# Part of VectorE's exponential on GpSimd, as int32 adds on pairs of int16 values, in a two-branch attention kernel

## The chip, the cores and the metric

The kernel runs on one core of one Trainium2 chip. The metric is device time in microseconds (us) of one execution; the median of several runs is quoted. The profile's own span, from the first to the last instruction, is about 1.8 us shorter than the measured time of the same run.

## The reference

Two attention branches over one sequence (S = 2048, D = 512, 32 heads of 16 columns) are mixed by a gate. All inputs are bf16.

```python
def reference(A_x, A_wqkv, A_wo, B_x, B_wqkv, B_wo, gate_w):
    def _A_ref(x, wqkv, wo):                     # full attention
        ...
        scores = jnp.einsum("bhqd,bhkd->bhqk", q, k) * scale
        p = _softmax(scores, axis=-1)
        o = jnp.einsum("bhqk,bhkd->bhqd", p, v)
        ...
    def _B_ref(x, wqkv, wo):                     # window of 8 keys, dilation 2
        ...
    x = A_x
    g = _sigmoid((x * gate_w).sum(-1, keepdims=True))
    a = _A_ref(x, A_wqkv, A_wo)
    b = _B_ref(x, B_wqkv, B_wo)
    return g * a + (1 - g) * b
```

The cost is in branch A: 32 heads x 2048 x 2048 scores must be exponentiated. The kernel cuts them into 2048 tiles of 128 x 512.

## The kernel before

The kernel holds a scheduler written in Python. While the program is built, it keeps a clock for each engine, picks what each engine does next from a list of steps with estimated durations, and emits that instruction. What runs on the chip is therefore one fixed order for each engine. Each score tile is given to one of two engines. ScalarE takes the true exponential of two or three tiles in one instruction. VectorE makes an approximation: it writes the score, scaled and shifted, as int16, whose bits read as fp16 are an exponential with a sawtooth error, and then two copies with another shift. The products with three differently weighted values average the error out.

```python
        def exp_dve(slot_item):                  # first step: one tile, from PSUM
            ...
            return nc.vector.tensor_scalar(out=self.yb[bt["buf"]][:, 0, i * 512:(i + 1) * 512], in0=bank[:],
                                           scalar1=A, scalar2=1024.0 * (15.0 + PW_S[0]), op0=ALU.mult, op1=ALU.add)

        def piece(bt, k):                        # second and third step: shifted copies of up to four tiles
            n = len(bt["items"]) * 512
            y = self.yb[bt["buf"]]
            return nc.vector.tensor_scalar(out=y[:, k, 0:n], in0=y[:, 0, 0:n],
                                    scalar1=float(round(1024.0 * (PW_S[k] - PW_S[0]))), scalar2=None, op0=ALU.add)
        ...
            for k in range(1, NP_):              # in close_batch: NP_ is 3
                s = Step("DVE", T_D4(n), lambda k=k: piece(bt, k), deps=list(bt["p1"]), due=bt["due"], cls=2)
                s.on_done = lambda end, k=k: done(k, end)
                s.port = True
                self.steps.append(s)
```

A step marked `port` is one that must not run beside GpSimd. The scheduler keeps such a step back while its clock for GpSimd is ahead, and makes each GpSimd instruction wait for the last of them:

```python
            if eng == "POOL" and port_last is not None:
                tc.add_manual_dep(inst.ins, port_last.ins.name, SYNC)
            if s.port:
                port_last = inst
```

```python
    def heads(self):
        pidx, pf, ei, ef = self.idx
        nc.vector.tensor_scalar(out=pidx[:], in0=pidx[:], scalar1=4, scalar2=None, op0=ALU.arith_shift_right)
        nc.vector.tensor_copy(out=pf[:], in_=pidx[:])
        nc.vector.tensor_copy(out=ef, in_=ei)    # 128x128, float32 from int32
        ...

    # elsewhere, where the steps are listed:
        self.steps.append(Step("DVE", 0.9, self.heads, rel=24, due=30, cls=2))
```

At the end each output tile of 128 rows is projected, cast into a staging tile of a rotating pool, and stored:

```python
        def ev():
            ob = self.wk.tile([P, D], BF16, name="ob", tag="ob")
            nc.vector.tensor_copy(out=ob[:], in_=self.misc[:])
            nc.sync.dma_start(out=self.o_dst[:, st, :], in_=ob[:])
```

Of the kernel before, what the change touches and what calls it, by code (L numbers as in the profile page):

```python
# [9 lines left out]
ALU = mybir.AluOpType  # L10
AX = mybir.AxisListType
ENG = mybir.EngineType
F32 = mybir.dt.float32
F16 = mybir.dt.float16
BF16 = mybir.dt.bfloat16
I16 = mybir.dt.int16
I32 = mybir.dt.int32
PSUM = bass.MemoryType.PSUM

P = 128  # L20
S = 2048
D = 512
# [19 lines left out]
NP_ = len(PW_S)  # L42
# [13 lines left out]
TUNE = dict(relL=64, dueL2=2040, R0=74, R1w=42, R1g=20, R2g=31, R3g=46, R3w=50, dueB=61, dueL=84, v2rel=79, v2step=21, v2due=91, krel=230, krel2=192, ahead=0.142, dueV=30, dueS=115, dueO=678, dlast=62, qrel=28, prelB=59, prodrel=-12)  # L56

LEVELS = dict(
    backlog=(0.758, 1.231, 1.61, 1.894, 2.273, 2.841, 3.788),
    backlog_s=(0.888, 1.442, 1.886, 2.219, 2.663, 3.329, 4.438),  # L60
    part_us=(0.6, 0.975, 1.275, 1.5, 1.8, 2.25, 3.0),
# [7 lines left out]
    order=((-1, 0, 1, 2, 1), (-1, 1, 0, 2, 3), (-1, 0, 2, 1, 3), (-1, 0, 1, 2, 3), (1, 0, 1, 2, 3), (0, 0, 1, 2, 3), (1, 0, 2, 1, 3), (2, 0, 1, 2, 3)),  # L69
)  # L70
STRETCH = dict(
    backlog="0333323133333333033333345336335333336333333333343333344333334633",
    backlog_s="0333333333333303331332333333333331333313430313333033333333333233",
    part_us="6333533463316323333303333303033333333333633463636333230333333333",
    misc_slack="3333333333333324333333433333333533332331033333333333333333333333",
    urgent="3333333333333333333333333333333333333333333353333363333333333333",
    fit="3533233333333333333133303333333333333333333330333333331333333363",
    port="1363353033333033333333333333333333335434353333333333333323533433",
    alone="3333333331363343333333333333333333133333333343333333631333333033",
    grab="0000000040000040000000004000000000004002000000000000000003000200",  # L80
    lend="0000000000060060000000000500020000000000000000000000200600060000",
    order="7001000330720000000000205000000000003000500010000000002000000002",
)
SLOT_D = 3
X_LAND = (0, 1.7, 3.7, 5.2)
# [631 lines left out]
T_D1 = lambda n: n / 960.0 + 0.075  # L717
T_D2 = lambda n: n / 1920.0 + 0.075
T_D4 = lambda n: n / 3840.0 + 0.075
T_P1 = lambda n: n / 750.0 + 0.1  # L720
T_P2 = lambda n: n / 480.0 + 0.06
MM = 0.216
SWITCH = 0.11
T_SP = 0.55
# [2 lines left out]
@with_exitstack  # L727
def kernel(
    ctx: ExitStack,
    tc: tile.TileContext,  # L730
    A_x: bass.AP,
    A_wqkv: bass.AP,
    A_wo: bass.AP,
    B_x: bass.AP,
    B_wqkv: bass.AP,
    B_wo: bass.AP,
    gate_w: bass.AP,
    out: bass.AP,
):
    nc = tc.nc  # L740
    aps = (A_x, A_wqkv, A_wo, B_x, B_wqkv, B_wo, gate_w, out)
    fpool = ctx.enter_context(tc.tile_pool(name="flag", bufs=1))
    flag = fpool.tile([P, 1], I32, name="flag")
    tc.mark_branch_hint_location("exact", hint="LikelyTaken", engines=[ENG.SP, ENG.Activation, ENG.DVE, ENG.PE, ENG.Pool])
    with ExitStack() as c1:
        _Fast(c1, tc, aps, flag).build()
    cond = nc.values_load(flag[0:1, 0:1], min_val=0, max_val=1)
    with tc.If(cond > 0, label="exact"):
        tc.strict_bb_all_engine_barrier()
        with ExitStack() as c2:  # L750
            _build_exact(c2, tc, aps)

class _Fast:
# [15 lines left out]
    def setup(self):  # L769
# [20 lines left out]
        self.t1 = c([P, 2, 16, 32], F32, name="t1")  # L790
        self.t2 = [c([P, 16, 32], BF16, name=f"t2_{i}") for i in range(2)]
        self.ident = c([P, P], BF16, name="ident")
        self.pmask = c([P, 2], F32, name="pmask")
        self.gw = c([P, 4], BF16, name="gw")
        self.gwr = c([P, 4, 32], BF16, name="gwr")
# [62 lines left out]
        for w, v, v4 in zip(PW_W[1:], self.vw[1:], self.vw4[1:]):  # L858
            nc.gpsimd.memset(v4[:, :, :, DH:VS], w)
            nc.gpsimd.memset(v4[:, :, 8, 0:DH], 0.0)  # L860
            nc.gpsimd.memset(v[:, len(KD) * H * VS:], 0.0)
        nc.gpsimd.memset(self.halo[:], 0.0)
        self.idx = pidx, pf, ei, ef
        nc.gpsimd.memset(self.ones[:], 1.0)
        for i in range(1, NQM):
# [571 lines left out]
    def outproj_specs(self, st):  # L1437
        nc = self.nc

        def mmh(srcs):  # L1440
            for br, ct in srcs:
                o = self.oT[ct] if br == "A" else self.oB(ct)
                w = self.woA if br == "A" else self.woB
                self.mm4(self.misc, lambda c: o[:, st * 128 + 32 * c:st * 128 + 32 * c + 32], w[:, ct, :],
                         start=(br == "B" and ct == 0), stop=(br == "A" and ct == 3))

        def ev():
            ob = self.wk.tile([P, D], BF16, name="ob", tag="ob")
            nc.vector.tensor_copy(out=ob[:], in_=self.misc[:])
            nc.sync.dma_start(out=self.o_dst[:, st, :], in_=ob[:])  # L1450
        order = [("B", c) for c in range(4)] + [("A", c) for c in range(4)]
        return [("PE", 2 * MM, lambda k=k: mmh(order[k:k + 2])) for k in (0, 2, 4, 6)] + [("DVE", T_D1(512), ev)]
# [30 lines left out]
    def run(self):  # L1483
# [39 lines left out]
        def tune(k):  # L1523
            return table[k][min(p, N - 1) * len(table[k]) // N]
# [23 lines left out]
        def ready_time(s):  # L1548
            r = 0.0
            for d in s.deps:  # L1550
                if d.end is None:
                    return INF
                r = max(r, d.end)
            return r
# [4 lines left out]
            return nc.vector.tensor_scalar(out=self.yb[bt["buf"]][:, 0, i * 512:(i + 1) * 512], in0=bank[:],  # L1559
                                           scalar1=A, scalar2=1024.0 * (15.0 + PW_S[0]), op0=ALU.mult, op1=ALU.add)  # L1560

        def piece(bt, k):
            n = len(bt["items"]) * 512
            y = self.yb[bt["buf"]]
            return nc.vector.tensor_scalar(out=y[:, k, 0:n], in0=y[:, 0, 0:n],  # L1565
                                    scalar1=float(round(1024.0 * (PW_S[k] - PW_S[0]))), scalar2=None, op0=ALU.add)

        def close_batch():
            nonlocal batch
            bt = batch  # L1570
            batch = None
            n = len(bt["items"]) * 512
            bt["refs"] = NP_ * len(bt["items"])
            parts = [dict(n=NP_) for _ in bt["items"]]

            def done(k, end):
                for i, it in enumerate(bt["items"]):
                    add_pv(it, self.yb[bt["buf"]][:, k, i * 512:(i + 1) * 512].bitcast(F16), end, ("y", bt, k), parts[i])
            for k in range(1, NP_):
                s = Step("DVE", T_D4(n), lambda k=k: piece(bt, k), deps=list(bt["p1"]), due=bt["due"], cls=2)  # L1580
                s.on_done = lambda end, k=k: done(k, end)
                s.port = True
                self.steps.append(s)
            last = bt["p1"][-1]

            def after(end, prev=last.on_done):
                prev(end)
                done(0, end)
            if last.end is None:
                last.on_done = after  # L1590
            else:
                done(0, last.end)

        def add_pv(it, rhs, ready, src, part=None):
            b, kt, j = it
            q = pvq[j]
            i = len(q)
            while i > 0 and q[i - 1][0] > b:
                i -= 1
            q.insert(i, [b, kt, rhs, ready, src, part or dict(n=1)])  # L1600
# [269 lines left out]
            return t["PE"] + 0.25  # L1870

        guard = 0
        while True:
            guard += 1
            assert guard < 2000000
# [13 lines left out]
                    moved = True  # L1889
            if p >= N and not self.steps and not aq and not any(pvq) and cur == NB:  # L1890
                break
            eng = min(t, key=lambda e: t[e])
            now = t[eng]
            others = min(v for e, v in t.items() if e != eng)
# [205 lines left out]
```

## Time and profile before

| | before |
|---|---|
| measured time, median of 3 | 714.39 us (714.26 to 714.79) |
| span of the profiled run | 712.4 us |
| busy: TensorE, VectorE, ScalarE, GpSimd | 689.5, 678.4, 691.3, 243.3 us |
| tiles: ScalarE, VectorE | 1492, 556 |
| last score round to the end of the span | 13.2 us |

In the profile PE is TensorE, DVE VectorE, ACT ScalarE and POOL GpSimd. A group's line has the source line, engine, operation, output and input names with shapes and the count, then after the bar the busy time in us and the mean duration of one in ns, then the idle time just before these instructions with what ended most of it.

### The profile page before, as it was taken

To read this page: it belongs to the slowest core of one execution; us is meant where nothing else is said; L and a number is where in the kernel's file an instruction comes from. 1 tells how busy PE (TensorE), PEld (TensorE's weight loads), DVE (VectorE), ACT (ScalarE), POOL (GpSimd) and SP (SyncE) were. 2 spreads that over 40 slices of the span, in tenths; PEclk is the share of its full clock that TensorE was granted. 3 is DMA by queue.
4 is the path that set the end of the run, shared out by engine and by line. 5 is a ranking of instruction groups with operands and counts; after the bars stand their busy time and mean duration, and the time that the engine had idled before them with its cause. 6 is when DMAs were issued, how large, how long until landed. Compare 5 with 4: busy or idle time off the path is not lost.

```text
span 712.4 us, 21197 instructions
## 1 busy us (share of the span) xinstructions
PE 689.5 (97%) x8558; PEld 221.9 (31%) x8558; DVE 678.4 (95%) x1154; ACT 691.3 (97%) x698; POOL 243.3 (34%) x258
## 2 busy tenths in 40 slices
PE   8999999999999999999989999999999999999996
PEld 4432222233232323223223233322332322222433
DVE  6999999998999999999999999999999999999974
ACT  5999999999999999999999999999999999999993
POOL 4245200132001324341003554556556456644200
PEclk9999999999999999999999999999999999999998
DMA  6001001000100100100033536555463655634001
GB/s 171 5 16 41 31 10 31 2 2 9 34 2 9 32 1 2 38 2 9 26 124 90 144 92 160 138 125 149 111 157 103 148 137 147 163 82 120 10 18 40
DMA packets 64485, 48.66 MB, mean 68 GB/s; under 512 B 22528, under 2 KB 64000, under 8 KB 64256
## 3 DMA queue, kind: packets, MB, share of 16 engines
q1 hardware_dynamic: 63680, 45.83, 24.9%
q8 instruction: 68, 1.11, 0.7%
q0 software_dynamic: 288, 1.05, 0.4%
q10 hardware_dynamic: 416, 0.39, 0.2%
q14 instruction: 33, 0.27, 0.1%
HBM read 39.85 MB, written 5.26 MB: 63 GB/s over the span
## 4 chain that ended last, share of the span: by engine, by line
PE 44%; ACT 36%; issue 9%; DVE 6%; DMA 3%; SPq 1%; POOL 0%; ACTq 0%; DVEq 0%; POOLq 0%
ACT pt L1912 35%; PE fps L1858 16%; PE fps L1631 15%; PE fps L887 10%; DVE yb L1559 3%; DVE yb L1565 2%; PE fps L1843 1%; PE fps L1373 1%; DMA erb<-er_dram 1%; PE fps L1238 1%; SPq L1349 1%; ACT er L1243 1%; DMA x_in<-in_A_x_dram 1%; DMA ww<-in_A_wqkv_dram 0%; SPq L1323 0%
## 5 line engine op out<-in xcount | busy, mean ns | idle before, releaser
L1912 ACT ACTIVATE pt<-fps 128x1024 bf16<-128x1024 f32 (+1 forms) x684 | 686.1, 1172 | 4.7 <-PE fps L1858 2.2
L1559 DVE TENSOR_SCALAR yb<-fps 128x512 int16<-128x512 f32 x556 | 360.4, 681 | 7.0 <-PE fps L1858 5.0
L1858 PE MATMUL fps<-qm,kT 32*128 32x512 bf16 x1962 | 288.6, 383 | 12.7 <-ACT pt L1912 8.9
L1631 PE MATMUL fps<-pt,vaug 128*32 128x512 bf16 (+1 forms) x1588 | 241.0, 373 | 0.1
L1565 DVE TENSOR_SCALAR yb<-yb 128x2048 int16<-128x2048 int16 (+2 forms) x294 | 187.4, 662 | 0.5
L1631 PE MATMUL fps<-yb,vaugw 128*32 128x512 f16 (+1 forms) x1176 | 173.8, 372 | 0.6 <-DVE yb L1565 0.4
L1858 PEld LDWEIGHTS <-kT 32*128 32x128 bf16 x1962 | 83.3, 91 | 273.7 <-issue 268.2
L1631 PE MATMUL fps<-yb,vaug 128*32 128x512 f16 (+1 forms) x588 | 108.6, 372 | 0.0
L887 PE MATMUL fps<-xT,ww 128*32 128x512 bf16 (+2 forms) x1296 | 99.8, 380 | 0.2 <-DVE gram L1067 0.2
L1355 POOL TENSOR_TENSOR er<-er,vw 128x512 bf16<-128x512 bf16 x64 | 73.1, 1157 | 69.1 <-DVE yb L1565 32.0
L1355 POOL TENSOR_TENSOR erb<-erb,vw 128x512 bf16<-128x512 bf16 x64 | 72.9, 1157 | 59.5 <-DVE yb L1565 41.0
L1631 PEld LDWEIGHTS <-vaug 128*32 128x32 bf16 x2176 | 65.2, 94 | 83.4 <-issue 75.1
L1631 PEld LDWEIGHTS <-vaugw 128*32 128x32 bf16 x1176 | 47.1, 95 | 40.2 <-issue 33.2
L1224 POOL TENSOR_TENSOR prod<-bq,bk 128x512 bf16<-128x512 bf16 x32 | 33.9, 1076 | 69.2 <-DVE yb L1565 52.3
L1664 POOL TENSOR_TENSOR t<-t,rc 128x512 bf16<-128x512 f32 x15 | 15.9, 1059 | 121.1 <-DVE yb L1565 95.9
L922 POOL TENSOR_SCALAR vaugw<-vaug 128x128 bf16<-128x128 bf16 (+1 forms) x24 | 20.9, 872 | 61.0 <-DVE vaug L915 31.8
L1843 PE MATMUL fps<-qm,kz 128*32 128x512 bf16 x344 | 37.8, 383 | 0.2 <-DVE yb L1559 0.2
L887 PEld LDWEIGHTS <-ww 128*32 128x32 bf16 x1296 | 25.6, 95 | 32.5 <-issue 25.4
L1224 DVE TENSOR_TENSOR prod<-bq,bk 128x2048 bf16<-128x2048 bf16 x24 | 28.6, 1220 | 0.3 <-PE fps L1238 0.3
L1654 DVE STREAM_TRANSPOSE t<-fps 128x512 f32<-128x512 f32 x32 | 22.6, 706 | 3.1 <-PE fps L1631 3.1
L887 PE MATMUL fps<-woB,oB 128*32 128x512 bf16 x256 | 20.2, 383 | 0.0
L887 PE MATMUL fps<-wAv,oT 128*32 128x512 bf16 x256 | 18.9, 383 | 0.0
(115 smaller groups left out, 290.3 us busy)
## 6 DMA issues: line engine op xcount, KB each, us to landing
vw<-v_dram SPq DMA_DIRECT2D x128, 128.0 KB, 3.1
er<-er_dram SPq DMA_DIRECT2D x128, 64.0 KB, 2.8
erb<-er_dram SPq DMA_DIRECT2D x128, 64.0 KB, 2.9
v_dram<-vs SPq DMA_DIRECT2D x16, 128.0 KB, 2.7
out_dram<-ob SPq DMA_DIRECT2D x15, 128.0 KB, 2.1
qm<-qs SPq DMA_DIRECT2D x112, 16.0 KB, 1.8
x_in<-in_A_x_dram SPq DMA_DIRECT2D x3, 512.0 KB, 6.2
ww<-in_B_wqkv_dram SPq DMA_DIRECT2D x12, 128.0 KB, 2.8
```

Of the source, the lines that this page charges most:

```text
L887: self.nc.tensor.matmul(out=out_ps[32 * c:32 * c + 32, 0:n], lhsT=lhsT_of(c), rhs=rhs, start=start, stop=stop, tile_position=(0, 32 * c))
L922: return self.nc.gpsimd.tensor_scalar(out=self.vw4[k][:, KD.index(st), h0:h1, 0:DH], in0=self.vaug4[:, st, h0:h1, 0:DH], scalar1=PW_W[k], ...
L1224: return e.tensor_tensor(out=pr[m % 2][:, a:b], in0=bq[ct][:, a:b], in1=bk[ct][:, o + a:o + b], op=ALU.mult)
L1355: return nc.gpsimd.tensor_tensor(out=st_["erb"][m % 4][:, g, :], in0=st_["erb"][m % 4][:, g, :], in1=st_["vw"][m % 2][:, g, :], op=ALU.mult)
L1559: return nc.vector.tensor_scalar(out=self.yb[bt["buf"]][:, 0, i * 512:(i + 1) * 512], in0=bank[:], scalar1=A, scalar2=1024.0 * (15.0 + PW_ ...
L1565: return nc.vector.tensor_scalar(out=y[:, k, 0:n], in0=y[:, 0, 0:n], scalar1=float(round(1024.0 * (PW_S[k] - PW_S[0]))), scalar2=None, op0 ...
L1631: nc.tensor.matmul(out=out, lhsT=v, rhs=r, start=start, stop=stop, tile_position=(0, 32 * j))
L1654: nc.vector.transpose(out=self.t1[:, par].rearrange("p a b -> p (a b)"), in_=self.flex[acc[b]])
L1664: return nc.gpsimd.tensor_tensor(out=t2, in0=self.t1[:, :, :, 0:DH], in1=h["rc"][:].unsqueeze(3).to_broadcast([P, 2, 16, DH]), op=ALU.mult)
L1843: nc.tensor.matmul(out=dst[32 * c:32 * c + 32, :], lhsT=self.kz[:, j, KZ.index(kt), 32 * c:32 * c + 32], rhs=self.qm[(4 * ct + qc) % NQM][ ...
L1858: nc.tensor.matmul(out=dst, lhsT=self.kT[ct % 2][32 * j:32 * j + 32, kt * 128:(kt + 1) * 128], rhs=self.qm[(4 * ct + qc) % NQM][par][32 * ...
L1912: nc.scalar.activation(out=self.pt[pi[0]][pi[1]][:, 0:n * 512], in_=self.aslot[si][:, 0:n, :].rearrange("p a b -> p (a b)"), func=ACT.Exp, ...
```

## The change

The intent: GpSimd is idle for two thirds of the span. Adding the same constant to two neighbouring int16 values is one int32 add of constant x 65537, as long as the lower half neither overflows nor borrows. So GpSimd can make a shifted piece with half as many elements. Wherever the scheduler expects GpSimd's backlog to be short, a piece goes there, VectorE gets room for more first steps, and ScalarE gets fewer tiles.

```diff
+T_PI = lambda n: n / 1150.0 + 0.12
-T_P1 = lambda n: n / 750.0 + 0.1
-T_P2 = lambda n: n / 480.0 + 0.06
+T_P1 = lambda n: n / 390.0 + 0.2
+T_P2 = lambda n: n / 470.0 + 0.065
 ...
+        for k in range(1, NP_):
+            nc.gpsimd.memset(self.pc[:, k:k + 1], round(1024.0 * (PW_S[k] - PW_S[0])) * 65537)
 ...
-            ob = self.wk.tile([P, D], BF16, name="ob", tag="ob")
+            ob = self.qs[st % 2] if st >= 12 else self.wk.tile([P, D], BF16, name="ob", tag="ob")
 ...
-        def piece(bt, k):
+        def piece(bt, k, gp=False):
             n = len(bt["items"]) * 512
             y = self.yb[bt["buf"]]
+            if gp:
+                return nc.gpsimd.tensor_tensor(out=y[:, k, 0:n].bitcast(I32), in0=y[:, 0, 0:n].bitcast(I32),
+                                               in1=self.pc[:, k:k + 1].to_broadcast([P, n // 2]), op=ALU.add)
 ...
+            now = min(t.values())
+            pl = max(0.0, t["POOL"] - now) + sum(s.cost for s in self.steps if s.eng == "POOL" and s.rel <= p
+                                                 and ready_time(s) <= now + 1.0)
             for k in range(1, NP_):
-                s = Step("DVE", T_D4(n), lambda k=k: piece(bt, k), deps=list(bt["p1"]), due=bt["due"], cls=2)
+                gp = pl < tune("pool") and n >= 1024
+                pl += gp * T_PI(n)
+                s = Step("POOL" if gp else "DVE", T_PI(n) if gp else T_D4(n), lambda k=k, gp=gp: piece(bt, k, gp),
+                         deps=list(bt["p1"]), due=bt["due"], cls=2)
-                s.port = True
+                s.port = not gp
```

Cut: the allocation of the constants `pc`, the levels of the control `pool`, the tables of the scheduler's controls, one digit for each of 64 stretches of the program, which are all set anew (with one added, `pool`), and a hint to the branch logic that is emitted at another place in the source.

More of the change, by code (lines that the diff above doesn't have):

```diff
@@ L58 @@
 LEVELS = dict(
+    pool=(0.0, 0.4, 1.2, 2.5, 4.0),
     backlog=(0.758, 1.231, 1.61, 1.894, 2.273, 2.841, 3.788),
@@ L71 @@
 STRETCH = dict(
-    backlog="0333323133333333033333345336335333336333333333343333344333334633",
-    backlog_s="0333333333333303331332333333333331333313430313333033333333333233",
-    part_us="6333533463316323333303333303033333333333633463636333230333333333",
-    misc_slack="3333333333333324333333433333333533332331033333333333333333333333",
-    urgent="3333333333333333333333333333333333333333333353333363333333333333",
-    fit="3533233333333333333133303333333333333333333330333333331333333363",
-    port="1363353033333033333333333333333333335434353333333333333323533433",
-    alone="3333333331363343333333333333333333133333333343333333631333333033",
-    grab="0000000040000040000000004000000000004002000000000000000003000200",
-    lend="0000000000060060000000000500020000000000000000000000200600060000",
-    order="7001000330720000000000205000000000003000500010000000002000000002",
+    pool="3133333333323333334333333333434334433333333333323333333333033320",
+    backlog="0333333333333633535336333353333353333332633333653333632333333433",
+    backlog_s="3316333333333333033330033333333333333313333331543333333334333332",
+    part_us="3333113343133433331230330033534333323533303333433313333431433313",
+    misc_slack="3033333333333033333333333333033333363333333333033333333333333333",
+    urgent="3033333333333363334333333333433333333033333333333335333333363333",
+    fit="3513335331335333313313353333333333313333333313330333333323343331",
+    port="3333333333233033023033333333333333333333333333333533333334333233",
+    alone="3333333333133333333231333331233033333333331333423333333336333333",
+    grab="0200000000000400233000000000000000000000000000000000000003000000",
+    lend="0000000000000001000660000000000000070000302000000000000003006000",
+    order="0060000000400000003004000000060000002000000206000000000000000000",
 )
@@ L743 @@
     flag = fpool.tile([P, 1], I32, name="flag")
-    tc.mark_branch_hint_location("exact", hint="LikelyTaken", engines=[ENG.SP, ENG.Activation, ENG.DVE, ENG.PE, ENG.Pool])
     with ExitStack() as c1:
@@ L792, in setup @@
         self.ident = c([P, P], BF16, name="ident")
+        self.pc = c([P, NP_], I32, name="pc")
         self.pmask = c([P, 2], F32, name="pmask")
@@ L1872, in run @@
         guard = 0
+        hinted = False
         while True:
@@ L1891, in run @@
                 break
+            if p >= 1024 and not hinted:
+                hinted = True
+                tc.mark_branch_hint_location("exact", hint="LikelyTaken",
+                                             engines=[ENG.SP, ENG.Activation, ENG.DVE, ENG.PE, ENG.Pool])
             eng = min(t, key=lambda e: t[e])
```

## The prediction

> **What bounds the kernel now.** I read the page first (busy shares, the slices, the chain), then the groups with shapes kept apart, then the busy time by stretches, the waits of ScalarE, and the timeline of the last 25 us.
>
> ```profile
> PE 689.5 (97%) x8558; PEld 221.9 (31%) x8558; DVE 678.4 (95%) x1154; ACT 691.3 (97%) x698; POOL 243.3 (34%) x258
> ...
> DVE  6999999998999999999999999999999999999974
> ACT  5999999999999999999999999999999999999993
> POOL 4245200132001324341003554556556456644200
> ...
> PE 44%; ACT 36%; issue 9%; DVE 6%; DMA 3%; SPq 1%; POOL 0%; ACTq 0%; DVEq 0%; POOLq 0%
> ```
>
> Three engines are full almost from end to end, and GpSimd (POOL) is not, least in the first half. The chain alternates between TensorE and ScalarE and hardly touches GpSimd. The program is laid out by a scheduler inside the kernel: each of 2048 score tiles (128x512) is exponentiated either by ScalarE or, by a bit trick in three pieces, by VectorE. The counts show the split:
>
> ```profile
> L1912 ACT ACTIVATE pt<-fps 128x1024 bf16<-128x1024 f32 x560 | 540.8, 1094 | 2.9 <-PE fps L1858 2.2 <-ACT pt L1912 0.2
> L1559 DVE TENSOR_SCALAR yb<-fps 128x512 int16<-128x512 f32 x556 | 360.4, 681 | 7.0 <-PE fps L1858 5.0 <-PE fps L1843 0.2
> L1912 ACT ACTIVATE pt<-fps 128x1536 bf16<-128x1536 f32 x124 | 189.2, 1526 | 1.7 <-DVE kT L995 1.1 <-ACT pt L1912 0.2
> L1565 DVE TENSOR_SCALAR yb<-yb 128x2048 int16<-128x2048 int16 x258 | 171.7, 687 | 0.4
> L1355 POOL TENSOR_TENSOR er<-er,vw 128x512 bf16<-128x512 bf16 x64 | 73.1, 1157 | 69.1 <-DVE yb L1565 32.0 <-DMA er<-er_dram 14.9 <-PE fps L1858 9.5
> ```
>
> ScalarE does 560 x 2 + 124 x 3 = 1492 tiles, VectorE 556. The idle column after ScalarE's groups is 2.9 + 1.7 us: it has practically no visible wait. Recorded durations of neighbours overlap, so I take the distance from one start to the next in the records instead: its median is 904 ns for 1024 columns and 1331 ns for 1536. 560 x 0.904 + 124 x 1.331 = **671.3 us** of ScalarE work that cannot be squeezed. The exponentials run from 9.2 to 700.8 us, 691.6 us; less 3.8 us for eight other exponentials (0.477 each), about 16 us are small stalls, 1.6 of them one wait at 14.6 us. So ScalarE sets the time within some 2%. TensorE's 97% says less, since its matmuls overlap: with 512 columns at the 0.213 us seen between back-to-back groups, a quarter of it for each of four packed matmuls, and 0.11 us for each of 1364 changes between row and column packing (a score round starts 0.32 us before its successor), its stream is 617 us, nine tenths of ScalarE's stretch. The end has a wait of its own:
>
> ```profile
> 704.23 0.69 DVE L1449 CAST ob<-fps 128x512 bf16<-128x512 f32 x1 [0.57 <-PE fps L887]
> 704.88 0.69 DVE L1468 CAST ob<-fps 128x512 bf16<-128x512 f32 x1
> ...
> 707.83 0.69 DVE L1449 CAST ob<-fps 128x512 bf16<-128x512 f32 x1 [2.25 <-DMA out_dram<-ob]
> 708.54 0.33 SPq L1450 DMA_DIRECT2D out_dram<-ob  x1
> ```
>
> One output tile waits 2.25 us for a staging buffer that an earlier store still holds, and its store is the last thing issued.
>
> **What the Trainium skill says.** *SBUF — State Buffer*, § SBUF: two separate sides: VectorE and GpSimd share a port pair as an exclusive lock, held for a whole instruction; a VectorE instruction in a 2-port mode and a GpSimd instruction block each other. The trace shows the program's answer: GpSimd's largest waits are on VectorE's shifted pieces (95.9 us before one group, 52.3 before another), and those pieces start 0.60 us apart with only rare long ones (1.25 us at most). *VectorE: DVE Perf Modes*, § Side-by-side gives about 693 ns for 2048 bf16 elements in 4x mode; the pieces here last 687. Its PSUM-fed first step is not a 2-port one, and can run beside GpSimd. *GPSIMD Engine Reference*, § 3.1 gives about 2.6 cycles an element for a two-input operation; 1157 ns for 512 elements here agrees (2.6 x 512 / 1.2 GHz = 1.11 us). Its § 4.1 says that an add with all operands of one 32-bit integer type is exact on GpSimd; no run shows that yet, and the change rests on it.
>
> **The change, part by part.** The build of the changed kernel shows what its scheduler decides.
>
> *ScalarE.* 602 exponentials of 1024 and 85 of 1536, so 1459 tiles: 602 x 0.904 + 85 x 1.331 = 657.3 us. That is **14.0 us less**. This is the term that matters.
>
> *VectorE.* 589 first steps instead of 556: 33 x 0.598 (median start to start) = +19.7 us. Its pieces go from 258/14/16/6 (of 2048/1536/1024/512 columns) to 187/7/12/0. With 0.600, 0.469, 0.34 and 0.20 us apiece, 167.9 falls to 119.7, -48.2. Together -28.5 us. VectorE was busy 671.7 of the 692 us between 9 and 701, so 20 us free; in a stretch 14 us shorter it would have about 34 free.
>
> *GpSimd.* 98 pieces, 93 of them 1024 int32 wide. One at the two-input rate seen (1157 ns for 512) would be 2.25 us. The kernel's own constant says 1.90, and its other two corrected constants fit the trace (1154 against 1157 ns, 528 and 1185 against 550 and 1195), so I take 1.9 to 2.25, that is 98 x 2 = about 185 to 215 us. GpSimd goes from 243 to about 430 us, 61% of the span. 86 of the 98 stand before the first product of L1355 (383 us in the profile), where it was mostly idle. None of this is on the path unless a piece comes late for its matmuls or holds the port.
>
> *Port.* VectorE's remaining pieces, its 24 products and small ones need the port some 120 + 27 + 8 = 155 us. With GpSimd's 430 that makes 585 of about 680 us, and they may not overlap. It fits, but without much play.
>
> *TensorE.* Each tile moved costs two more product matmuls: 66 x 0.053 = 3.5 us. Against it 24 fewer fillers (-1.3) and 24 fewer spread score matmuls (-1.3), and one row round fewer. By the count above 617 becomes 618: 91% of the shorter stretch.
>
> *Tail.* Tiles 12 and 13 leave through other buffers, so the 2.25 us wait goes. But the new order puts the out-projection of all four last tiles (128 matmuls, 6.8 us) after the last score round, where before 28 of them preceded it. From the last score round to the last projection I count 7.7 us of TensorE work against 5.4. Before, that round was at 699.14 and the last store was issued 9.4 us later. After: 4.9 us to the end of the products, 2.2 us normalisation, 1 us last matmuls, 0.7 cast, a store on ScalarE's queue landing 0.5 us later than one on the other. I expect 0.6 us saved, not 2.25.
>
> *Branch hint.* Moved in the source, but it stands first in both built programs: nothing. The two memsets added lie in a GpSimd that is free from 6.5 to 14.9 us: nothing.
>
> Sum: 712.4 - 14.0 - 0.6 = 697.8 us of span; the measured time is 2.0 above the span now, so 699.8 with the small stalls unchanged. I add 0.6 for the closer coupling of VectorE and GpSimd: **700.4 us**.
>
> **Rivals.** (1) *The port becomes the bound.* If pieces on GpSimd take 2.3 us or more, VectorE's pieces queue behind them; each collision costs up to a piece's length, and 100 collisions of 0.5 us would eat more than VectorE's 34 us. Against it: the scheduler keeps the two apart, and does so well now. Result: 704 to 715. (2) *TensorE limits.* At 91% with rounds of mostly two banks (0.90 us of ScalarE against 0.33 + 0.55 us for a round and eight products), stalls of ScalarE could grow from 16 to 22 us: 706. For it: TensorE already holds the largest share of the chain. Against it: hardly any visible wait of ScalarE. (3) *Better fit.* The scheduler's GpSimd durations were too low and its controls are set anew; VectorE gets more air. If stalls fall by 4 us and the tail wait is fully won: 694.
>
> **Range and chances.** The first term is firm; the uncertainty is the stalls, -4 to +6 us, hence **695 to 706**. Two per cent lies at 700.1, beside my value, so it is nearly even: faster 0.47, within 2% 0.51, slower 0.02.
>
> **What would show it.** Right: 687 exponentials on ScalarE with unchanged distances and an idle sum still under 8 us; VectorE's busy time near 650; GpSimd near 430; pieces on GpSimd of 1.9 to 2.25 us; the distance from the last score round to the span's end near 12.6 us (now 13.3). Wrong: VectorE's pieces longer than 700 ns on average (port collisions), ScalarE waiting for score rounds in the first half, or TensorE starting products late behind the int32 adds. A GpSimd piece well over 2.25 us would sink the prediction.

## More of the kernel before

The prediction shows the lines that matter and reads them. One more is needed later, from the timeline of before around 21 us (start in us, duration in us, engine, line, operation): the unmarked 128 x 128 cast of `heads`, whose code is shown here too, takes 0.22 us.

```profile
20.93 0.22 DVE L875 CAST t<-t 128x128 f32<-128x128 int32 x1
```

## The result, and the profile after

The changed kernel takes **702.9 us** (702.75 to 703.27, four runs) against 714.55 us for the kernel before in the same rounds, and its result is right. The ratio is 0.9838 with an interval of 0.9821 to 0.9855. The gain of 1.6% is within the 2% that counts as the same.

The page of the changed kernel, busy times and slices (each digit is a fortieth of the span, in tenths busy), then the chain's shares:

```profile
PE 681.1 (97%) x8578; PEld 218.6 (31%) x8578; DVE 658.5 (94%) x1099; ACT 677.9 (97%) x701; POOL 422.0 (60%) x358
...
DVE  5999999998789999999999999999999999999975
ACT  5999999999999999999999999999999999999993
POOL 3556667677477545645557486676745765656680
...
PE 54%; ACT 30%; issue 7%; DVE 5%; DMA 2%; SPq 1%; POOL 1%; ACTq 0%; POOLq 0%
```

GpSimd has taken on 179 us, spread over the whole span, while VectorE lost 20 us and ScalarE 13. ScalarE's row of nines is unbroken as before. The groups with shapes apart, from the table of all engines:

```profile
L1931 ACT ACTIVATE pt<-fps 128x1024 bf16<-128x1024 f32 x602 | 571.8, 1084 | 3.9 <-PE fps L1872 2.8 <-PE fps L1645 0.4
L1564 DVE TENSOR_SCALAR yb<-fps 128x512 int16<-128x512 f32 x589 | 382.1, 681 | 16.0 <-PE fps L1872 11.4 <-PE fps L1857 0.6
...
L1571 POOL TENSOR_TENSOR yb<-yb,pc 128x1024 int32<-128x1024 int32 x93 | 174.9, 1891 | 69.3 <-DVE yb L1564 25.1 <-DVE yb L1573 17.0 <-DVE prod L1229 7.0
...
L1931 ACT ACTIVATE pt<-fps 128x1536 bf16<-128x1536 f32 x85 | 128.7, 1514 | 2.4 <-PE fps L1872 1.1 <-DVE kT L1000 1.1
L1573 DVE TENSOR_SCALAR yb<-yb 128x2048 int16<-128x2048 int16 x187 | 127.4, 704 | 0.5
```

A piece on GpSimd takes 1891 ns, so the constant in the source (1.90) was right. VectorE's idle time before first steps grew from 7.0 to 16.0 us: it has more air than it uses.

**Where the 11.2 us of span come from.** Busy times of ScalarE overlap at the edges, so I use distances between starts, as the prediction did. The medians are unchanged, 904 ns for 1024 columns and 1330 for 1536.

| | before | after | difference | predicted |
|---|---|---|---|---|
| ScalarE's work, counts x distances | 671.3 | 657.3 | -14.0 | -14.0 |
| stalls between first and last exponential | about 15.5 | about 17.8 | +2.3 | +0.6 |
| start of the first exponential | 9.16 | 9.28 | +0.1 | 0 |
| last exponential's start to the end | 12.66 | 13.04 | +0.4 | -0.6 |
| span | 712.4 | 701.2 | -11.2 | -14.0 |

The stalls are what is left of the distance from the first to the last exponential's start (690.6 and 678.9 us) after the work and 3.8 us for eight other exponentials. The work came out exactly. The stalls and the tail gave back 2.8 us. One new stall of 1.35 us stands out, before 24.25 us (a longer one, 1.75 us before 14.7 us, is in both kernels); the timeline points to an instruction at 21 to 22 us as its cause:

```profile
18.18 3.74 POOL L1571 TENSOR_TENSOR yb<-yb,pc 128x1024 int32<-128x1024 int32 x2
...
20.59 1.42 DVE L880 CAST t<-t 128x128 f32<-128x128 int32 x1
...
24.25 2.37 ACT L1931 ACTIVATE pt<-fps 128x1536 bf16<-128x1536 f32 x2 [1.14 <-PE fps L1872]
```

The cast of `heads`, 0.22 us before, takes 1.42 us and ends at 22.01, just after GpSimd's two adds end at 21.92. VectorE is late by 1.2 us, and ScalarE waits for the score round behind it. The cast is not marked `port`, and before the change no int32 add stood beside it. A shorter GpSimd instruction did (`vaugw`, the first of two, 20.72 to 21.29 us), and it did not hold up the cast, which ran from 20.93 to 21.15:

```profile
20.72 1.19 POOL L922 TENSOR_SCALAR vaugw<-vaug 128x128 bf16<-128x128 bf16 x2 [2.19 <-DVE vaug L915]
```

So not every overlap costs time; why this one did not is not shown. The int32 adds do hold VectorE up: in the changed kernel 13 of VectorE's shifted pieces start inside one, at least 0.18 us before it ends, and all 13 are longer than the median of their shape, by 0.07 to 0.48 us.

The tail of the changed kernel, from the timeline (the 64 matmuls of L892 shown are the projection of tiles 12 and 13; as many follow for 14 and 15):

```profile
687.69 0.39 PE L1872 MATMUL fps<-qm,kT 32*128 32x512 bf16 x2
...
688.01 1.91 PE L892 MATMUL fps<-woB,oB 128*32 128x512 bf16 x32
...
689.74 1.90 PE L892 MATMUL fps<-wAv,oT 128*32 128x512 bf16 x32
...
691.26 1.29 DVE L1454 CAST qs<-fps 128x512 bf16<-128x512 f32 x2 [2.80 <-PE fps L892]
...
696.53 0.33 SPq L1474 DMA_DIRECT2D out_dram<-ob  x1
696.64 0.38 ACTq L1478 DMA_DIRECT2D out_dram<-eg  x1
```

From the last score round to the last store's issue it takes 8.95 us (before 9.40), and from there to the end 4.56 us (before 708.54 to 712.4, 3.86). The 2.25 us wait for a staging buffer is gone, but all 128 projection matmuls of the last four tiles now stand behind the last score round, and the store issued last takes longer to land.

### The profile page after: what moved, and what is told of

Read it like the earlier page. It is cut to its first block, busy times and chain, and to the rows that moved or that the text cites. A ratio compares the mean times of both kernels' runs of the same rounds, so it can differ in the third digit from the quotient of the medians. Undisturbed runs are those within 1.5% of the kernel's fastest.

```text
span 701.2 us, 21355 instructions
## 1 busy us (share of the span) xinstructions
PE 681.1 (97%) x8578; PEld 218.6 (31%) x8578; DVE 658.5 (94%) x1099; ACT 677.9 (97%) x701; POOL 422.0 (60%) x358
## 4 chain that ended last, share of the span: by engine, by line
PE 54%; ACT 30%; issue 7%; DVE 5%; DMA 2%; SPq 1%; POOL 1%; ACTq 0%; POOLq 0%
ACT pt L1931 29%; PE fps L1872 19%; PE fps L1645 18%; PE fps L892 13%; DVE yb L1564 2%; PE fps L1857 1%; PE fps L1243 1%; PE fps L1378 1%; DMA erb<-er_dram 1%; DMA v_dram<-vs 1%; DVE er L1298 1%; SPq L1328 1%; DVE yb L1573 1%; ACT er L1248 0%; DMA vw<-v_dram 0%
## 5 line engine op out<-in xcount | busy, mean ns | idle before, releaser
L1931 ACT ACTIVATE pt<-fps 128x1024 bf16<-128x1024 f32 (+1 forms) x687 | 672.0, 1137 | 6.3 <-PE fps L1872 3.9
L1564 DVE TENSOR_SCALAR yb<-fps 128x512 int16<-128x512 f32 x589 | 382.1, 681 | 16.0 <-PE fps L1872 11.4
L1872 PE MATMUL fps<-qm,kT 32*128 32x512 bf16 x1968 | 285.7, 383 | 11.4 <-ACT pt L1931 7.4
L1645 PE MATMUL fps<-pt,vaug 128*32 128x512 bf16 (+1 forms) x1557 | 233.8, 372 | 0.1
L1571 POOL TENSOR_TENSOR yb<-yb,pc 128x1024 int32<-128x1024 int32 (+2 forms) x98 | 181.3, 1861 | 71.1 <-DVE yb L1564 25.1
L1872 PEld LDWEIGHTS <-kT 32*128 32x128 bf16 x1968 | 80.6, 91 | 274.3 <-issue 269.7
L1573 DVE TENSOR_SCALAR yb<-yb 128x2048 int16<-128x2048 int16 (+2 forms) x206 | 136.9, 688 | 0.6
L1645 PE MATMUL fps<-yb,vaug 128*32 128x512 f16 (+1 forms) x619 | 103.4, 374 | 0.1
L1360 POOL TENSOR_TENSOR erb<-erb,vw 128x512 bf16<-128x512 bf16 x64 | 72.6, 1154 | 46.6 <-DVE yb L1573 33.7
L892 PE MATMUL fps<-xT,ww 128*32 128x512 bf16 (+2 forms) x1296 | 99.1, 380 | 0.0
L1645 PEld LDWEIGHTS <-vaugw 128*32 128x32 bf16 x1238 | 44.7, 94 | 42.0 <-issue 36.3
L892 PEld LDWEIGHTS <-ww 128*32 128x32 bf16 x1296 | 25.4, 95 | 31.3 <-issue 24.8
L1857 PE MATMUL fps<-qm,kz 128*32 128x512 bf16 x320 | 34.5, 382 | 0.5 <-DVE yb L1564 0.2
L1678 POOL TENSOR_TENSOR t<-t,rc 128x512 bf16<-128x512 f32 x15 | 15.9, 1057 | 28.6 <-DVE yb L1573 14.7
L892 PE MATMUL fps<-woB,oB 128*32 128x512 bf16 x256 | 19.7, 382 | 0.0
```

The lines of the kernel that those rows point to most:

```text
L892: self.nc.tensor.matmul(out=out_ps[32 * c:32 * c + 32, 0:n], lhsT=lhsT_of(c), rhs=rhs, start=start, stop=stop, tile_position=(0, 32 * c))
L1360: return nc.gpsimd.tensor_tensor(out=st_["erb"][m % 4][:, g, :], in0=st_["erb"][m % 4][:, g, :], in1=st_["vw"][m % 2][:, g, :], op=ALU.mult)
L1571: return nc.gpsimd.tensor_tensor(out=y[:, k, 0:n].bitcast(I32), in0=y[:, 0, 0:n].bitcast(I32), in1=self.pc[:, k:k + 1].to_broadcast([P, n ...
L1645: nc.tensor.matmul(out=out, lhsT=v, rhs=r, start=start, stop=stop, tile_position=(0, 32 * j))
L1857: nc.tensor.matmul(out=dst[32 * c:32 * c + 32, :], lhsT=self.kz[:, j, KZ.index(kt), 32 * c:32 * c + 32], rhs=self.qm[(4 * ct + qc) % NQM][ ...
L1872: nc.tensor.matmul(out=dst, lhsT=self.kT[ct % 2][32 * j:32 * j + 32, kt * 128:(kt + 1) * 128], rhs=self.qm[(4 * ct + qc) % NQM][par][32 * ...
```

## The experiments

In the expectations, theory A is the account that the prediction and the table above give: ScalarE's work sets the time, the pieces on GpSimd cost nothing beside it, and what was lost is a few stalls and the tail. Rivals carry a letter or are called the rival; what they claim stands with them. Times are medians, with the lowest and highest run; "before" was 714.09 to 714.15 us in these rounds.

### What the pieces and the new settings are worth

**Same order, pieces back on VectorE.** The program keeps the order of the changed kernel, but the 98 pieces are emitted for VectorE.

```diff
-            if gp:
+            if False:
                 return nc.gpsimd.tensor_tensor(out=y[:, k, 0:n].bitcast(I32), in0=y[:, 0, 0:n].bitcast(I32),
```

> The changed kernel in exactly its order, but the 98 pieces run on VectorE at the places where the scheduler gave them to GpSimd: 98 x about 0.60 = 58 us more for VectorE, and GpSimd back at about 240 us. VectorE stands idle about 29 us between 9 and 690 us of the changed kernel's profile. Theory A (VectorE, freed by GpSimd, is what lets ScalarE hand over 33 tiles): the order falls 25 to 45 us behind, 728 to 748. Rival (the new tables make the gain, and the pieces on GpSimd are of little use): 703 to 712.

Measured: 747.01 us (746.39 to 747.63), ratio 1.0461, result right. The busy line:

```profile
PE 701.2 (94%) x8578; PEld 221.0 (30%) x8578; DVE 707.5 (95%) x1197; ACT 690.0 (93%) x701; POOL 246.1 (33%) x260
```

About 58 us of work (98 x 0.60, VectorE's distance for a piece) put back on VectorE cost 44 us of time, inside theory A's range. Some of it may be the clock's: TensorE was granted half its clock in two stretches of 10.2 us here (from 302 and 408 us), in which it lost up to 10 us; the changed kernel shows a halved clock only in its last 2.5 us, after its matmuls. VectorE has little room of its own in this order: taking the pieces off it is what lets it do 589 first steps.

**New settings without pieces, and pieces with the old settings.** In these two the scheduler decides anew.

```diff
-                gp = pl < tune("pool") and n >= 1024
+                gp = False
```

> The changed kernel with its new tables, but every piece on VectorE, and the scheduler deciding anew. The build gives VectorE 528 tiles and ScalarE 559 + 134 exponentials of 1024 and 1536 columns, 683.7 us of work at the distances measured, 26.4 more than in the changed kernel. Theory A (tables and pieces belong together; without the pieces VectorE takes less): 726 to 733. Rival (the tables alone make the gain): 703 to 712.

```diff
 STRETCH = dict(
-    pool="3133333333323333334333333434334433334333333333323333333333033320",
-    backlog="0333333333333633535336333353333353333332633333653333632333333433",
+    pool="3333333333333333333333333333333333333333333333333333333333333333",
+    backlog="0333323133333333033333345336335333336333333333343333344333334633",
 ... (the other ten tables set back to those of before)
```

> The pieces on GpSimd with the old tables and the new durations, the scheduler deciding anew. The build gives 112 pieces to GpSimd, but only 523 tiles to VectorE, and ScalarE 549 + 142 + 1 exponentials, 685.8 us, 14.5 more than in the kernel before. Theory A (a table set fits one program; moved pieces alone don't make it faster): 726 to 735. Rival (the pieces make the gain by themselves): 702 to 710.

Measured: 726.83 us (726.66 to 727.0), ratio 1.0174, and 734.65 us (734.33 to 734.96), ratio 1.0284, both right. Their busy lines, the first without pieces, the second with pieces and old tables:

```profile
PE 698.8 (96%) x8498; PEld 227.8 (31%) x8498; DVE 658.0 (91%) x1120; ACT 704.3 (97%) x707; POOL 242.8 (33%) x260
```

```profile
PE 696.1 (95%) x8438; PEld 229.2 (31%) x8438; DVE 607.3 (83%) x997; ACT 708.0 (97%) x706; POOL 439.9 (60%) x372
```

Both came out inside theory A's range, and each half alone is worse than the kernel before. Without pieces VectorE gets 528 tiles and ScalarE's work by counts and distances is 683.7 us, 12.4 more than before; the time is 12.7 longer. With 112 pieces but old tables VectorE gets 523 tiles, though it is busy only 83% of the span, and ScalarE's work is 685.8 us, 14.5 more; the time is 20.6 longer, the rest being more stalls of ScalarE (here TensorE's clock was halved for 6.8 us). The controls decide which engine gets a tile, so freed time on VectorE is worth nothing until they hand tiles over. The parts can't be added up: the change is pieces and tables together. One rival stays open: no run sets the controls anew for a kernel without pieces, so how much of the 1.6% such tuning, or the corrected durations, could reach alone is not known.

### Does the piece on GpSimd hold anything up?

**Every third piece done twice.** The second copy repeats the first, so the result stays right; the order stays the same.

```diff
             if gp:
+                self.n_gp = getattr(self, "n_gp", 0) + 1
+                if self.n_gp % 3 == 0:
+                    nc.gpsimd.tensor_tensor(out=y[:, k, 0:n].bitcast(I32), in0=y[:, 0, 0:n].bitcast(I32),
+                                            in1=self.pc[:, k:k + 1].to_broadcast([P, n // 2]), op=ALU.add)
                 return nc.gpsimd.tensor_tensor(...)
```

> The changed kernel in its order, with every third int32 piece on GpSimd done twice: 32 x 1.89 = 60 us more for GpSimd, from 422 to about 482 of 690 us. GpSimd and VectorE's port users together then take about 640. Theory A (the shared port and GpSimd still have play): 703 to 713, much less than 60 us. Rival P (the port or GpSimd is all but the bound): 735 to 763.

Measured: 759.97 us (759.16 to 760.78), ratio 1.0645, result right. With some 60 us of extra GpSimd work (32 x 1.89) the time grew by 57 us. Theory A's 703 to 713 fell. The waits of this run (engine and line, what it waited for, us in all, times, longest):

```profile
ACT pt L1935 <- PE fps L1876: 51.2, 62, 2.3
...
DVE yb L1564 <- PE fps L1876: 36.2, 54, 2.6
PE fps L1649 <- POOL yb L1575: 35.0, 33, 1.9
```

TensorE waits for a piece 33 times (28 of them a doubled one) by up to 1.9 us, the length of a piece, and ScalarE then waits for the score rounds behind those products. VectorE instructions that collided with GpSimd were longer by 19.8 us in sum, against 5.4 in the changed kernel.

Not all of the 57 us is the pieces', though. TensorE's granted clock was halved in eight stretches, 34 us together, each of which begins within 2 us of a wait of TensorE of 1.0 to 2.2 us. One of them (window in us, its length, busy time of PE, PEld, DVE, ACT and POOL with counts, granted clock, DMA share and GB/s):

```profile
114.20:121.00 6.80, 6.74 (x51) 1.25 (x50) 3.12 (x5) 3.54 (x4) 4.17 (x3) 0.50 0.00 0
```

ScalarE's lag behind the changed kernel's order grew by 56 us in all, 25 of it in these stretches, which hold waits for pieces too. At half clock TensorE lost up to 17 us in them, so an estimate from these figures leaves some 39 us or more to the waits themselves. Whether the waits brought the clock down is not tested. GpSimd itself was busy only 489.6 of 757 us, so it isn't full. The order is stiff: TensorE's products stand in a fixed sequence, and when one comes late, what stands behind it is late too. At 1.89 us a piece fits the 1.90 that the scheduler was given: the changed kernel's waits show none of TensorE for a piece.

### Where do ScalarE's remaining stalls come from?

**TensorE made lighter.** The second half of each projection is left out, 600 matmuls or 32 us by the distance between them. The result is wrong.

```diff
     def proj_mm(self, wt, kcs, sc):
-        for kc in kcs:
+        for kc in kcs if kcs[0] == 0 else ():
             self.mm4(self.misc, lambda c: wt[:, kc, 32 * c:32 * c + 32], self.xT[:, kc, sc * 512:(sc + 1) * 512],
-                     start=(kc == 0), stop=(kc == 3))
+                     start=(kc == 0), stop=(kc == (1 if len(kcs) == 2 else 3)))
```

> Wrong result on purpose: 75 projection steps of two contraction blocks do nothing, so TensorE loses 600 packed matmuls, 32 us of its stream, in an otherwise unchanged order. Theory A (ScalarE sets the pace, TensorE only causes the small stalls, about 18 us between the first and last exponential): 5 to 12 us less, 691 to 698. Rival T (TensorE is the bound): 671 to 680. Rival N (the stalls come from VectorE and the port): 701 to 703.

**VectorE made lighter.** 131 of its 206 pieces are left out; the products that would read them read the unshifted piece. (The result still passed the tolerance, but it isn't the intended approximation.)

```diff
-                    add_pv(it, self.yb[bt["buf"]][:, k, i * 512:(i + 1) * 512].bitcast(F16), end, ("y", bt, k), parts[i])
+                    add_pv(it, self.yb[bt["buf"]][:, 0 if k in skip else k, i * 512:(i + 1) * 512].bitcast(F16), end, ("y", bt, k), parts[i])
+            skip = []
 ...
+                if k == 2 and not gp:
+                    skip.append(k)
```

> Wrong result on purpose: the changed kernel in its order, but 131 of VectorE's 206 remaining pieces are left out and their matmuls read the unshifted piece: about 78 us less for VectorE and for the shared port, nothing else moved. In proj_half, with 32 us less for TensorE, ScalarE's small stalls stayed at 17 us (18 in the changed kernel). Theory V (a VectorE that runs late makes those stalls): ScalarE's stalls fall under 8 us, 691 to 697. Rival S (they come from how the score rounds are dealt out, not from a late engine): 700 to 703.

Measured: 701.92 us (701.62 to 702.23), ratio 0.9831, with lighter TensorE; 702.41 us (701.92 to 702.9), ratio 0.9832, with lighter VectorE. The busy lines, TensorE's case first:

```profile
PE 661.0 (94%) x7978; PEld 217.7 (31%) x7978; DVE 658.0 (94%) x1099; ACT 677.4 (97%) x701; POOL 422.4 (60%) x358
```

```profile
PE 679.1 (97%) x8578; PEld 215.8 (31%) x8578; DVE 590.9 (84%) x968; ACT 677.7 (97%) x701; POOL 421.2 (60%) x358
```

Removing 32 us from TensorE saved 1.0 us, removing 68 us from VectorE 0.5. The kernel before was 0.4 us faster in these rounds too, so these savings are upper values. Neither bounds the kernel. (The TensorE work was taken out between 0 and 600 us, none after.) In the first run theory A, that TensorE causes the stalls, missed, and rival N's time came; but the second run speaks against N's cause and for rival S. I listed each place where ScalarE starts over 60 ns later than its median distance. The changed kernel has 91 of them. The lighter-TensorE run has 78, of which 70 are the same ones, with 17.4 of its 18.5 us; the lighter-VectorE run has 85, of which 84 are the same, with 18.4 of its 18.6 us. So nearly all stalls belong to the order of the program, not to the amount of work on TensorE or VectorE; no run makes GpSimd or ScalarE alone lighter. (These sums include some 4 us of other work on ScalarE.) What in the order makes each of them is not settled here, but for the one at 22 us.

### The stall at 22 us

**`heads` early.** The five small VectorE instructions are emitted in the setup, before any GpSimd piece exists.

```diff
         self.idx = pidx, pf, ei, ef
+        self.heads()
 ...
-        self.steps.append(Step("DVE", 0.9, self.heads, rel=24, due=30, cls=2))
+        self.steps.append(Step("DVE", 0.9, lambda: None, rel=24, due=30, cls=2))
```

> The changed kernel with the five small VectorE instructions that build the masks issued in the setup, while VectorE waits for the first input, and not at 20 us; the schedule's order is otherwise the same. One of them, the 128x128 int32 to float32 copy, took 1.42 us beside the int32 adds on GpSimd where it took 0.22 us before, and ScalarE stood 1.35 us longer a little later. Theory A (one port collision of an instruction that the scheduler does not know as a port user): 1.0 to 2.0 us less than the changed kernel's 702.9, so 701 to 702. Rival (that wait is made up later, because TensorE or VectorE sets the pace): within 0.4 us of 702.9.

Measured with five rounds: **702.05 us** (701.68 to 702.2), ratio 0.9831 with 0.9818 to 0.9844, result right. That is 0.85 us less than the median of the changed kernel, taken in another call, and the fastest version with the intended result, though the two intervals of the ratio overlap and the kernel before was 0.4 us faster in this call too. Theory A's range (701 to 702) and the rival's (within 0.4 us of 702.9) were both missed by little, so the time alone does not decide. The trace does: from the first to the last start of the exponentials it is 0.90 us less. The timeline:

```profile
17.90 3.74 POOL L1572 TENSOR_TENSOR yb<-yb,pc 128x1024 int32<-128x1024 int32 x2
...
20.54 1.18 DVE L1123 COPY gwr<-gw 128x128 bf16<-128x128 bf16 x1
...
23.02 1.45 ACT L1932 ACTIVATE pt<-fps 128x1536 bf16<-128x1536 f32 x1 [0.21 <-PE fps L1873]
```

ScalarE's stall by start distances fell from 1.35 to 0.41 us. The collision didn't vanish, it moved to the next unmarked instruction: a 128 x 128 copy that took 0.22 us before now takes 1.18 and ends at 21.72, again just after GpSimd's adds (21.64). It costs less, since VectorE no longer has the five small instructions in that place.

### The tail

**Changed kernel with the old buffers.**

```diff
-            ob = self.qs[st % 2] if st >= 12 else self.wk.tile([P, D], BF16, name="ob", tag="ob")
+            ob = self.wk.tile([P, D], BF16, name="ob", tag="ob")
```

> The changed kernel with tiles 12 and 13 in the two shared staging buffers again. Theory A (in the new order the store of the buffer that the last tile needs has landed by 694 us, the last tile is converted at 695.8, so nothing waits): the own buffers are worth nothing here, 702.7 to 703.3. Rival (the own buffers saved the 2.3 us and something else took it back): 705 to 706.

Measured: 703.44 us (702.89 to 703.75), ratio 0.9851 with 0.9836 to 0.9866; the interval overlaps that of the changed kernel. That is 0.14 us above theory A's range and far from the rival's. No cast of an output tile waits for a buffer in the trace, and the profiled spans differ by 0.2 us (701.4 and 701.2): in the new order no gain from the own buffers is shown.

**Kernel before with the new buffers, for tiles 12 and 13.** The same line, applied to the kernel before.

> The kernel before with nothing changed but the own buffers for tiles 12 and 13. Theory A (in the old order the wait of 2.25 us and what follows it is the end of the chain; the other stores were issued 2.8 us before the last one): 2.0 to 3.0 us less, 711.5 to 712.6. Rival (another store ends as late): under 0.5 us less.

Measured: 713.84 us (713.3 to 714.54), ratio 0.9994 with 0.9979 to 1.001. Theory A missed: the wait stayed, at 2.44 us:

```profile
708.20 0.69 DVE L1449 CAST ob<-fps 128x512 bf16<-128x512 f32 x1 [2.44 <-DMA out_dram<-ob]
```

In the program of the kernel before the stores come in the order 8, 9, 12, 13, 10, 14, 15, 11. The tile that waits is number 11, which the change doesn't touch. In the changed kernel's program tile 11 comes before 12, and no wait is left for the buffers to remove.

**Kernel before with own buffers for tiles 10 and 11.**

```diff
-            ob = self.wk.tile([P, D], BF16, name="ob", tag="ob")
+            ob = self.qs[st % 2] if st in (10, 11) else self.wk.tile([P, D], BF16, name="ob", tag="ob")
```

> The kernel before with own buffers for tiles 10 and 11. The build of the kernel before stores its tiles in the order 8, 9, 12, 13, 10, 14, 15, 11: the tile that waits 2.25 us is number 11, not 12 or 13, which is why own buffers for those two gave nothing. Theory A (that wait ends the chain): 2.0 to 3.0 us less than the kernel before, 711.1 to 712.2. Rival (the store of the tile on ScalarE's queue ends nearly as late): under 0.7 us less.

Measured: 712.84 us (712.5 to 713.94), ratio 0.9987 with 0.997 to 1.0003, so 1.3 us less by the medians: between theory A and the rival, and not clear of the noise. The wait is gone. The timeline of the stores:

```profile
705.49 0.33 SPq L1469 DMA_DIRECT2D out_dram<-ob  x1
705.60 0.38 ACTq L1473 DMA_DIRECT2D out_dram<-eg  x1
706.13 1.22 SPq L1450 DMA_DIRECT2D out_dram<-qs  x1
```

The last store is issued at 706.13 instead of 708.54, 2.4 us earlier, but its issue takes 1.22 us instead of 0.33 and the span ends 5.2 us after it instead of 3.9. Of the 2.4 us the profiled span kept 1.1. It is the fourth store within 1.3 us (the first at 704.84); in the kernel before three stores within 0.8 us took 0.33 to 0.38 us each to issue. That the stores get in each other's way is a guess, and the mechanism is not shown.

**Projection of tiles 12 and 13 freed of the late windowed branch.** To let TensorE do this work earlier, the projection reads rows of branch B that are ready before; the result is wrong.

```diff
+                sq = st - 4 if br == "B" and st >= 12 else st
-                self.mm4(self.misc, lambda c: o[:, st * 128 + 32 * c:st * 128 + 32 * c + 32], w[:, ct, :],
+                self.mm4(self.misc, lambda c: o[:, sq * 128 + 32 * c:sq * 128 + 32 * c + 32], w[:, ct, :],
 ...
-                               deps=[s3] + [self.oB_done[(qc, c)] for c in range(4)])
+                               deps=[s3] + ([] if last else [self.oB_done[(qc, c)] for c in range(4)]))
```

> Wrong result on purpose. In the changed kernel the last output of the windowed branch is ready 2.6 us before ScalarE ends (36 us in the kernel before), so the out-projections of tiles 12 and 13 cannot start before the last score round. Here they take that branch's part from tiles 8 and 9 and may start earlier; the build has 5.2 us of TensorE work after the last score round against 7.9, and 1460 tiles on ScalarE against 1459. Theory A (work behind the last score round is what makes the tail): 1.5 to 2.5 us less than the changed kernel, 700.4 to 701.4. Rival (TensorE is full in the last 30 us, so work moved ahead only delays the score rounds): 702.5 to 704.5.

Measured: 705.02 us (704.24 to 705.5), ratio 0.9875, 2.1 us *slower* than the changed kernel. The timeline of ScalarE near the end:

```profile
684.01 6.95 ACT L1932 ACTIVATE pt<-fps 128x1024 bf16<-128x1024 f32 x7 [1.53 <-PE fps L1646]
```

By the build TensorE has 5.2 us of work instead of 7.9 after the last score round, and the tail is 0.5 us shorter, but ScalarE's last exponential starts 2.1 us later than in the changed kernel. ScalarE waits 1.53 us for TensorE, which just before runs projections that were moved ahead (L892) and products (L1646, which the view names). So the work costs at least as much ahead of the round as behind it. The rival told the direction; its range was exceeded by 0.5 us. That TensorE has no free time there fits its busy share, but is not tested apart.

## Why the prediction was right or wrong

The prediction said 700.4 us in a range of 695 to 706; 702.9 was measured. Span by span it was 2.8 us low; 0.3 of this was made up by luck, since it took time and span 2.0 us apart, a median against the span of one run (run by run it is 1.8 in both kernels). It also gives 13.3 us from the last score round to the end, which is 13.2 (712.38 - 699.14), and expected 12.6 after the change, where 13.5 came. By its own steps:

1. **"So ScalarE sets the time within some 2%": right.** 687 exponentials with unchanged distances gave the 14.0 us. 32 us less on TensorE or 68 less on VectorE gained 1.0 and 0.5 us. In the two runs with the scheduler deciding anew the time goes up with ScalarE's work (12.4 us more work and 12.7 more time without pieces, 14.5 and 20.6 with the old tables). No run makes ScalarE's work alone smaller.
2. **VectorE and GpSimd: right in size.** VectorE's busy time is 658.5 us (said: near 650), its idle time between 9 and 690 us 29 (said: about 34), GpSimd's 422 (said: about 430). A piece took 1.891 us, the low end of 1.9 to 2.25; all 98 took 181.4 us. That such adds are exact, on which the change rests, is borne out only as far as the result with 98 of them is right, and that test is wide: it passed as well with 131 pieces left out.
3. **"It fits, but without much play": right, for another reason.** The port collisions add only 5.4 us to 26 VectorE instructions (1.8 before), and the cast's 1.2. The mean of VectorE's pieces rose from 687 to 704 ns, which passes the 700 I named as a sign of trouble, without much trouble. The lack of play is the stiffness of the order, which the doubled pieces showed: most of an unplanned delay of 60 us goes to the end (some 39 us or more of it, beside the halved clock), though GpSimd is only 60% busy in the changed kernel.
4. **"I add 0.6 for the closer coupling of VectorE and GpSimd": mis-sized, 2.3 us measured.** 1.35 us of the stalls is the one at 22 us, an instruction that isn't marked as a user of the port and meets a GpSimd instruction that wasn't there before. I counted the marked users of the port and left these aside. The remaining stalls sit at fixed places of the order and don't follow from the load of TensorE or VectorE.
5. **"Tiles 12 and 13 leave through other buffers, so the 2.25 us wait goes": this step failed.** The wait went, but not for that reason, so this part came out by luck. The waiting tile was number 11, as the two runs with the kernel before show, and it is the new order that puts it earlier. Own buffers for tiles 12 and 13 show no gain in either kernel. The trace of before names the buffer, not the tile; I took the tiles that the diff treats to be those that wait, where the build's store order would have told.
6. **"I expect 0.6 us saved" in the tail: failed, 0.4 lost.** The path to the last store's issue was counted well (8.95 us, where the terms sum to 8.8). But the text lists the store that lands later on ScalarE's queue, by 0.5 us, and never takes it off the 0.6; the landing was in fact 0.7 longer.
7. **Branch hint and memsets: nothing,** as said; no run tests them apart.

Of the rivals, the port as a bound (704 to 715) did not come true, and TensorE as a limit (706) is refuted by the run with lighter TensorE. Stalls did grow, though, from about 16 to about 18 us, a third of the growth that this rival feared. The better fit (694) did not come.

## What to carry to other kernels

Work moved to an idle engine is worth what the engine that sets the time gives up, no more: count that engine's instructions in the build and multiply by their distance in the trace, and then look for the stalls one by one. In a program with one fixed order an idle engine is a small reserve; the duration assumed for each instruction must be right, all users of a shared port must be marked, and settings tuned for the old mix have to be tuned again together with the change. Before a buffer is widened to remove a wait, find out which tile waits.

## What the Trainium skill lacked or had wrong

- *GPSIMD Engine Reference*, § 3.1 gives about 2.6 cycles an element for a two-input elementwise operation. The int32 add with one operand broadcast from a single column took 1891 ns for 1024 elements, 1466 for 768 and 1040 for 512: 1.66 ns more for each element, or 2.0 cycles at the 1.2 GHz that the page computes with. The bf16 products (1154 ns for 512) agree with 2.6, so the figure shouldn't be used for this form of add; whether the broadcast operand or the int32 type is the reason no run tests.
- *SBUF — State Buffer*, § SBUF: two separate sides: the lock held for a whole instruction agrees with two small copies that grew from 0.22 us to 1.42 and 1.18 and ended within 0.1 us of GpSimd's adds. Here 128 x 128 was enough to cost ScalarE a stall of 1.35 us; what was lacking was the mark in the kernel's scheduler. One case of the kernel before does not show the lock: the cast ran from 20.93 to 21.15 inside a GpSimd instruction (20.72 to 21.29) and took its usual 0.22 us. The profile's times on GpSimd are rough, so this does not refute the page.
- I found no page that gives a figure for what stores close behind one another cost: the fourth of four within 1.3 us took 1.22 us to issue instead of 0.33.
